# Two weight-chunk scalings moved to other places in VectorE's stream, and the first row tile normalized in two pieces

## The chip, the cores, the metric

One core of a Trainium2 chip. The metric is the device time of one execution in microseconds (us); medians of several executions are quoted. All kernels gave correct results.

## The reference

```
xn = layernorm(x)                                  # x: 2048 x 640, bf16
q  = xn @ wq                                       # 640 x (32 heads x 192)
s  = softmax(q @ k^T / sqrt(192)) @ v              # the last 512 keys of each head
s  = s @ wo                                        # (32 x 192) x 640
g  = silu( (sigmoid(xn @ w_gate) * (xn @ w_up)) @ w_down )
out = x + s * g
```

## The kernel before

The kernel computes the gated block first (from about 15 us), then the query projection of the first head group (from 164 us), then score and value phases of one head group after another, and the output products at the end. Query weights are cut into five chunks per group (one per 128 rows of wq). Before a chunk of the second group can be used it is scaled by one instruction, on VectorE for the chunks that matter here, and then combined into four sums by GpSimd:

```python
def scale_raw(g, c, on_act=True):
    raw = raw_t[g, c][:]
    if on_act:
        nc.scalar.activation(raw.bitcast(F16), raw, AF.Copy, scale=w_up)
    else:
        nc.vector.tensor_scalar(raw.bitcast(F16), raw, w_up, None, op0=ALU.mult)   # the row L221

def second_w(c):                                   # all of it on GpSimd
    copy_w(1, c, nc.gpsimd.tensor_copy)
    sum_w(1, c, nc.gpsimd.tensor_tensor, nc.gpsimd.tensor_copy)
    load_raw(1 + (c + 3) // NCD, (c + 3) % NCD, nc.gpsimd)
```

Where these stand in the stream is decided by two loops. `slots` are the parts of the first query projection; `stage_s` is one score tile, and `q_list` holds the next group's query parts that are woven between the score tiles:

```python
for n, k in enumerate((0, 1, 7, 2, 3, 8, 4, 5, 9, 6, 10)):
    slots[k]()
    ...
    elif n == 6:
        scale_raw(1, 2, on_act=False)              # third chunk: amid the projection
    if n in (0, 1, 6):
        second_w(min(n, 2))
...
        for k, x in enumerate(s_list):             # 16 score tiles
            stage_s(r, *x, k)
            ...
            if r == 0 and k in (3, 7):             # fourth and fifth chunk
                scale_raw(1, 3 + k // 4, on_act=False)
                second_w(3 + k // 4)
```

The normalization of a row tile is one VectorE instruction (`tensor_scalar`, 128x640), ahead of five transposes on TensorE.

All sixteen row tiles end in `finish`, which takes an output buffer from a pool of four ("fout"), multiplies by the gate, adds, and writes to HBM. Of the last eight some have their addition on GpSimd, and the last of all is done in three pieces (comments added in this cut and the ones above):

```python
def finish(ps, gB_sb, t, d0, d1, on_pool=False, queue=nc.sync):
    o_sb = late["fout"].tile([P, D], BF16, name="o_sb")      # "fout": 4 buffers in turn
    d = slice(d0, d1)
    if on_pool:
        tmp = late["tmp"].tile([P, D], F32, name="tmp")
        nc.vector.tensor_tensor(tmp[:, d], ps, gB_sb[:, d], ALU.mult)
        nc.gpsimd.tensor_tensor(o_sb[:, d], tmp[:, d], acc[t][:, d], ALU.add)
    else:
        nc.vector.tensor_tensor(ps, ps, gB_sb[:, d], ALU.mult)       # last multiplication
        nc.vector.tensor_tensor(o_sb[:, d], ps, acc[t][:, d], ALU.add)   # last addition
    queue.dma_start(of[t * P:(t + 1) * P, d], o_sb[:, d])
```

Each call takes the next buffer of the ring. The third piece of the last row tile therefore gets the buffer of the fourth user before it, a whole row tile whose addition was on GpSimd, and its own addition waits until that tile's 160 KB are written (in the profile before they land 1.78 us after the issue, at 899.48 us, and the addition starts at 899.66).

The softmax here doesn't subtract the row's maximum and nothing guards it: scores larger than these inputs give would overflow.

## Time and profile before

| | kernel before |
|---|---|
| time, median of 3 runs | 905.09 us (904.78 to 905.09) |
| span of the profiled run | 902.9 us |
| busy: TensorE, VectorE, ScalarE, GpSimd | 99%, 72%, 48%, 20% |
| first product of the gated block | 14.80 us |
| first query product, second score phase | 164.18 us, 209.63 us: 45.45 us apart |

The lines that carry this are in the prediction below. One view that I did not show there, because I did not look at it closely enough, is the chain of work that ended last, in order of time. Its end in the kernel before (start, duration, what):

```profile
896.13 1.55 POOL o_sb L726
897.68 0.02 issue
897.70 1.78 DMA out_dram<-o_sb
899.48 0.03 DVEq L729
...
899.66 0.29 DVE o_sb L729
```

The last addition is released by an output write, not by TensorE. The margin is small: in VectorE's timeline the last multiplication starts 0.45 us before it.

```profile
899.21 0.29 DVE L728 TENSOR_TENSOR ps_all<-ps_all,gBa_sb 128x128 f32<-128x128 f32 x1
899.66 0.29 DVE L729 TENSOR_TENSOR o_sb<-ps_all,acc_hi 128x128 bf16<-128x128 f32 x1 [0.16 <-DVE ps_all L728]
```

### The profile page before, as it was taken

How to read it: one execution, taken by the hardware profiler on the slowest of the kernel's cores; microseconds unless marked ns; L12 is line 12 of the kernel's file. 1: busy time of each engine (PE TensorE's matmuls, PEld its weight loads, DVE VectorE, ACT ScalarE, POOL GpSimd, SP SyncE). 2: the span in 40 equal slices, each digit the busy share in tenths (PEclk: the TensorE clock that was granted, in tenths of full speed). 3: DMA queues.
4: the chain of work that ended last, by engine and by line, in shares of the span. 5: the costliest groups of instructions: out<-in, count | busy, mean ns of one | idle time of the engine just before them, and what ended most of it. 6: DMA issues, size and time to landing. Idle time of an engine off the chain costs nothing. (4 is left out here: it accounts for less than half of the span.)

```text
span 902.9 us, 18554 instructions
## 1 busy us (share of the span) xinstructions
PE 896.0 (99%) x7791; PEld 531.6 (59%) x7791; DVE 653.0 (72%) x1090; ACT 432.9 (48%) x511; POOL 178.8 (20%) x220
## 2 busy tenths in 40 slices
PE   9999999999999999999999999999999999999998
PEld 5545454556656565656565656566666666565665
DVE  5879956677677867786778677866786678666566
ACT  4323346764247633753376437643854285424240
POOL 0051112780001100110011001100110000001982
PEclk9999999999999999999999999999999999999999
DMA  9993384424554645373626362727293815263744
GB/s 284 269 268 92 97 146 104 119 55 87 87 91 59 144 76 102 60 143 69 109 56 147 57 119 46 157 54 123 31 172 45 132 23 129 39 120 130 159 128 121
DMA packets 188069, 100.38 MB, mean 111 GB/s; under 512 B 156176, under 2 KB 180368, under 8 KB 187984
## 3 DMA queue, kind: packets, MB, share of 16 engines
q1 hardware_dynamic: 158656, 57.69, 32.5%
q0 software_dynamic: 9408, 29.93, 14.2%
q10 hardware_dynamic: 19920, 11.57, 5.5%
q8 instruction: 61, 1.00, 0.5%
q14 instruction: 24, 0.20, 0.1%
HBM read 57.87 MB, written 5.24 MB: 70 GB/s over the span
## 5 line engine op out<-in xcount | busy, mean ns | idle before, releaser
L657 ACT ACTIVATE E<-ps_all 128x1024 bf16<-128x1024 f32 x256 | 252.7, 1022 | 303.0 <-PE ps_all L653 184.8
L714 PE MATMUL ps_all<-wo_g,oT 128*128 128x512 bf16 (+2 forms) x1542 | 228.3, 299 | 0.0
L653 PE MATMUL ps_all<-qT,kT 64*128 64x512 bf16 x1536 | 194.4, 376 | 0.0
L671 PE MATMUL ps_all<-v_sb,E 128*128 128x193 bf16 x2048 | 189.8, 247 | 0.1
L671 PEld LDWEIGHTS <-E 128*128 128x128 bf16 x2048 | 168.6, 98 | 18.7 <-issue 6.8
L714 PEld LDWEIGHTS <-oT 128*128 128x128 bf16 x1542 | 121.5, 98 | 78.4 <-issue 2.3
L584 DVE COPY qp<-ps_all 128x512 f32<-128x512 f32 x150 | 100.7, 688 | 58.4 <-PE ps_all L563 58.3
L601 DVE TENSOR_TENSOR qT<-ps_all,qp 128x512 bf16<-128x512 f32 x165 | 109.7, 688 | 45.7 <-PE ps_all L563 37.4
L653 PEld LDWEIGHTS <-kT 64*128 64x128 bf16 x1536 | 75.4, 94 | 89.2 <-issue 5.2
L678 DVE TENSOR_TENSOR o_st<-ps_all,rden 128x768 bf16<-128x768 f32 x120 | 114.9, 957 | 5.0 <-DMA oT<-o_st 0.9
L202 POOL DMA_DIRECT2D raw<-in_A_wq_dram x80 | 48.1, 606 | 276.2 <-ACT wB L224 238.9
L135 POOL DMA_DIRECT2D k_sb<-in_A_k_cache_dram x32 | 32.7, 1026 | 275.2 <-DVE o_st L678 155.6
L219 ACT ACTIVATE raw<-raw,w_sc 128x1536 f16<-128x1536 bf16 x37 | 58.3, 1575 | 1.9 <-DMA raw<-in_A_wq_dram 1.0
L497 PE MATMUL ps_all<-wd_sb,hT_sb 128*128 128x512 bf16 (+1 forms) x384 | 52.8, 299 | 0.0
L563 PE MATMUL ps_all<-XA,wA 64*128 64x512 f16 x420 | 51.9, 376 | 0.2 <-DVE qp L584 0.2
L563 PE MATMUL ps_all<-XB,wB 64*128 64x512 f16 x420 | 52.0, 376 | 0.0
L563 PE MATMUL ps_all<-X,w 64*128 64x512 bf16 x420 | 51.9, 376 | 0.0
L749 DVE TENSOR_TENSOR acc_lo<-ps_all,acc_lo 128x640 f32<-128x640 f32 x48 | 39.5, 823 | 15.9 <-PE ps_all L714 15.7
L453 DVE TENSOR_TENSOR hT_sb<-ps_all,sig_sb 128x512 bf16<-128x512 f32 x48 | 32.4, 683 | 22.0 <-ACT sig_sb L452 11.3
L677 DVE RECIPROCAL rden<-ps_all 128x4 f32<-128x4 f32 x128 | 23.2, 181 | 34.1 <-PE ps_all L671 32.7
L452 ACT ACTIVATE sig_sb<-ps_all 128x512 bf16<-128x512 f32 x48 | 28.0, 596 | 40.1 <-PE ps_all L447 37.1
L749 DVE TENSOR_TENSOR acc_hi<-ps_all,acc_hi 128x640 f32<-128x640 f32 x48 | 39.3, 819 | 7.7 <-PE ps_all L714 7.7
(118 smaller groups left out, 764.0 us busy)
## 6 DMA issues: line engine op xcount, KB each, us to landing
raw<-in_A_wq_dram POOLq DMA_DIRECT2D x80, 192.0 KB, 4.1
k_sb<-in_A_k_cache_dram POOLq DMA_DIRECT2D x32, 192.0 KB, 5.6
wo_g<-in_A_wo_dram ACTq DMA_DIRECT2D x6, 960.0 KB, 7.1
v_sb<-in_A_v_cache_dram ACTq DMA_DIRECT2D x28, 192.0 KB, 3.8
gB_d<-gB_sb POOLq DMA_DIRECT2D x16, 160.0 KB, 3.5
gBa_sb<-gB_d SPq DMA_DIRECT2D x16, 160.0 KB, 3.9
xa_sb<-in_A_x_dram SPq DMA_DIRECT2D x16, 160.0 KB, 3.9
out_dram<-o_sb SPq DMA_DIRECT2D x15, 160.0 KB, 1.9
```

The lines of the kernel that those rows point to most:

```text
L202: eng.dma_start(raw[r], wq_r[:, c, :, g * GC:(g + 1) * GC])
L219: nc.scalar.activation(raw.bitcast(F16), raw, AF.Copy, scale=w_up)
L497: nc.tensor.matmul(oB_ps[:, d0:d0 + dsz], lhsT=hT_sb[:, f, q * P:(q + 1) * P], rhs=wd_sb[:, f, d0:d0 + dsz], start=(f == 0), stop=(f == NF ...
L563: nc.tensor.matmul(ps_all[:, b, :], lhsT=w(r, c), rhs=x[r, c, :], start=(first and k == 0), stop=(k == len(cs) - 1), skip_group_check=True,)
L584: nc.vector.tensor_copy(dst, part(b))
L601: nc.vector.tensor_tensor(q_out(i, u, pp), part(b), t, ALU.add)
L653: nc.tensor.matmul(ps[:, b, :], lhsT=kT[h, c * PC + j, :], rhs=qT_t[r][i, j][h, pp, :], start=(j == 0), stop=(j == PC - 1),)
L657: nc.scalar.activation(E_t[r, i, pp][:, c, :, :], ps, AF.Exp, scale=scale_qk)
L671: nc.tensor.matmul(o_ps[:, q // 2, q % 2, 0:DH + 1], lhsT=E[:, c, h, q * P:(q + 1) * P], rhs=vt[:, c, 0:DH + 1], start=(c == 0), stop=(c = ...
L678: nc.vector.tensor_tensor(o_st[:, :, h * DH:(h + 1) * DH].rearrange("p (b i) d -> p b i d", b=2), o_ps[:, :, :, 0:DH], rden[:].to_broadcas ...
L714: nc.tensor.matmul(oA[:, d0 - base:d0 - base + dsz], lhsT=oT_t[r, i, pp][:, q * PC + j, :], rhs=wo_t[runs[r][1]][:, cc, d0:d0 + dsz], star ...
L749: nc.vector.tensor_tensor(acc[t][:], oA[:, 0:D], acc[t][:], ALU.add)
```

## The change

Its intent: take the scalings of the third and fifth chunk away from places where TensorE waits for VectorE right behind them, and let TensorE's first transposes start before the whole first row tile is normalized. The line numbers of the changed kernel are 2 higher than before in what follows it (L563 becomes L565, L729 becomes L731).

```diff
         def ln_apply(t):
             xn = xpool.tile([P, D], BF16, name="xn")
-            nc.vector.tensor_scalar(
-                xn[:], x_tiles[t], mv[:, t, 0:1], rstd[:, t, :],
-                op0=ALU.subtract, op1=ALU.mult,
-            )
+            cuts = [0, 2 * P, D] if t == 0 else [0, D]
+            for d in map(slice, cuts, cuts[1:]):
+                nc.vector.tensor_scalar(
+                    xn[:, d], x_tiles[t][:, d], mv[:, t, 0:1], rstd[:, t, :],
+                    op0=ALU.subtract, op1=ALU.mult,
+                )
             return xn
@@
-        elif n == 6:
-            scale_raw(1, 2, on_act=False)
-        if n in (0, 1, 6):
-            second_w(min(n, 2))
+        if n < 2:
+            second_w(n)
+    scale_s = {0: 2, 3: 3, 15: 4}
@@
-            if r == 0 and k in (3, 7):
-                scale_raw(1, 3 + k // 4, on_act=False)
-                second_w(3 + k // 4)
+            if r == 0 and k in scale_s:
+                scale_raw(1, scale_s[k], on_act=False)
+                second_w(scale_s[k])
```

## The prediction

> **What bounds the kernel now.** I read the page first (busy shares, slices, the chain that ended last), then the waits of TensorE, then the timeline of the two stretches that the diff touches: the query projection and first score phase (164 to 211 us) and the head (1 to 12 us).
>
> The page: TensorE is busy 896.0 of 902.9 us, in every slice, at full granted clock. The slice row and the engine row say the same thing from two sides.
>
> ```profile
> span 902.9 us, 18554 instructions
> PE 896.0 (99%) x7791; PEld 531.6 (59%) x7791; DVE 653.0 (72%) x1090; ACT 432.9 (48%) x511; POOL 178.8 (20%) x220
> PE   9999999999999999999999999999999999999998
> PEclk9999999999999999999999999999999999999999
> ```
>
> So the change can give back only gaps on TensorE. The waits of TensorE name four. The third and fourth belong to the query products; the first two to the head.
>
> ```profile
> PE ps_all L350 <- DVE warm L344: 1.3, 1, 1.3
> PE ps_all L563 <- DVE qT L601: 0.4, 1, 0.4
> PE ps_all L360 <- ACT X L375: 0.3, 1, 0.3
> PE ps_all L563 <- DVE qp L584: 0.2, 1, 0.2
> ```
>
> These idle figures are too small, because the ends of matmuls are modelled and stretch into the gap; starts are the safe thing to subtract. In the timeline of TensorE, ten half-height matmuls take 1.08 us from start to start and twelve take 1.29 or 1.30 (next fence, a later score phase of the same shape, with nothing in its way).
>
> ```profile
> 223.02 1.24 PE L563 MATMUL ps_all<-X,acc_hi 64*128 64x512 bf16 x10
> 224.10 1.46 PE L653 MATMUL ps_all<-qT,kT 64*128 64x512 bf16 x12
> 225.40 1.24 PE L563 MATMUL ps_all<-XA,acc_hi 64*128 64x512 f16 x10
> ```
>
> Now the stretch of the change: the timeline of VectorE and TensorE, with the two scaling instructions of L221 that the diff moves.
>
> ```profile
> 172.01 1.29 DVE L601 TENSOR_TENSOR qT<-ps_all,acc_lo 128x512 bf16<-128x512 f32 x2 [3.07 <-PE ps_all L563]
> 173.22 0.61 DVE L221 TENSOR_SCALAR raw<-raw,w_sc 128x1536 f16<-128x1536 bf16 x1
> 173.74 3.08 DVE L601 TENSOR_TENSOR qT<-ps_all,acc_lo 128x512 bf16<-128x512 f32 x5
> ...
> 173.90 1.33 PE L563 MATMUL ps_all<-XC,wC 64*128 64x512 bf16 x10
> 175.68 0.80 PE L563 MATMUL ps_all<-XC,wC 64*128 64x512 bf16 x5 [0.45 <-DVE qT L601]
> ...
> 190.66 1.26 DVE L221 TENSOR_SCALAR raw<-raw,w_sc 128x1536 f16<-128x1536 bf16 x1
> 191.84 0.68 DVE L584 COPY qp<-ps_all 128x512 f32<-128x512 f32 x1
> ...
> 190.92 1.47 PE L653 MATMUL ps_all<-qT,kT 64*128 64x512 bf16 x12
> 192.57 1.25 PE L563 MATMUL ps_all<-XA,wA 64*128 64x512 f16 x10 [0.18 <-DVE qp L584]
> ```
>
> Gap one: the ten products start at 173.90, so the split ones could start at 173.90 + 1.08 = 174.98; they start at 175.68, 0.70 late. Gap two: 190.92 + 1.30 = 192.22 against 192.57, 0.35 late. Both stand right behind a scaling on VectorE that sits ahead of a read of PSUM for which TensorE is waiting.
>
> [...] the three scalings have one shape, yet take 0.61, 0.89 and 1.26 us. At 173.22 GpSimd was issuing loads; the one at 190.66 met a GpSimd product that ran from 190.59 to 191.50, and 191.50 + 0.42 is its end.
> [...] The wait at 175.68 is that: the split product writes the bank that the first add of the preceding slot reads.
> [...] The trace before has no cut one of this kind; its 128x640 normalization takes 0.44 us and lets the next instruction start after 0.36 (4.72 to 5.08).
>
> **The change part by part.** Count of work: VectorE gets one instruction more, all else keeps its count; the order of instructions on TensorE, ScalarE and GpSimd does not change. Everything is a matter of where three waits end.
>
> Third chunk, from the middle of the projection to the first score tile. Without the scaling at 173.22 the five adds behind it, which start every 0.60 us, can follow the two at 172.01 directly. The third add waits for TensorE (171.74 + 1.08 for its ten products, + 0.20 us until TensorE's end is seen = 173.02) and for VectorE, free at 172.01 + 1.20 = 173.21. So the adds start at 173.21, 173.81, 174.41 where they started at 173.74, 174.34, 174.94. The one at 174.41 reads the bank of the split product; it ends 0.69 later, 175.10, and TensorE goes on 0.05 later (as 175.63 led to 175.68): 175.15. Gain 0.53 us; 0.17 of the gap stays, because the adds themselves are behind. What follows hangs on the split product: it runs 0.65, ScalarE copies one half (0.60), VectorE adds (0.69), and the first product of the next tile waits for that add; before, 175.68 led to 177.75, 2.07 us, where TensorE alone needs 0.65 + 1.30 = 1.95. I keep the 2.07: 177.22. So 0.53 is passed on whole.
> The scaling itself now falls behind the last add, at about 177.1. VectorE is idle there: the row of the copy at 179.03 says 1.32 us before it. A scaling of 0.61, or up to 1.26 if it meets GpSimd, must be done by 179.03 - 0.53 = 178.50; in the worse case it meets a GpSimd copy that ends at 177.60 and ends at about 178.1. Cost 0. GpSimd needs the chunk at 181.12, so that doesn't wait either.
>
> Fourth chunk: stays behind the fourth score tile (183.69, 0.89 us), no gain. Moving 0.53 earlier it meets GpSimd at another point, at worst ending near 184.6; the two copies behind it then end at 185.8, and TensorE wants those banks at 186.38 - 0.53 = 185.85. Cost 0, by a hair.
>
> Fifth chunk, from behind the eighth score tile to behind the sixteenth. The 1.26 us at 190.66 are gone, the copy at 191.84 starts at about 190.66, and TensorE no longer waits: gain 0.35. At its new place VectorE has done its last add at about 199.45 - 0.88 = 198.57, and the first reciprocal of the value phase comes at 200.47 - 0.88 = 199.59, after 1.02 us of idle time in the row before. GpSimd has nothing to do then (it waits for this very chunk), so the scaling takes 0.61: 199.2, hidden. GpSimd's own five products and copies of this chunk slip from 195.80 to about 199.2 and, at 5.9 us for a chunk, end near 205.1; the load behind them is issued by 206.4. TensorE first reads the chunk in the next score phase, which starts at 209.63 - 0.88 = 208.75, some 2 us into it (fifth of five chunks). Margin over 4 us. Cost 0.
>
> First row tile in two pieces of 256 and 384. The intent is that TensorE's first two transposes begin before the whole row is normalized. Starts of the head, from its timeline: normalization 4.72, transposes 5.23, two warming products 5.74, first real product 6.54; the chain on VectorE and ScalarE beside it: statistics 5.08, aggregate 5.61, square root 5.85, copy of the turned tile 6.05 (0.36 us for the first part). The first piece may end 0.1 to 0.2 us before 5.17. The copy on ScalarE is behind the square root of the second tile, which is behind the statistics that VectorE does after both pieces, so it gets not earlier but later[...]. Then the wait of TensorE at 8.54 (0.26 us, for the copy of the second tile) moves later by as much. But the head has two anchors behind it: VectorE waits 0.53 us for a row tile at 8.11, which doesn't move, and TensorE's transposes at 9.21 wait for what VectorE does after it, while TensorE's products before them end at 8.54 + 10 x 0.056 = 9.10. So 0.11 us of delay is swallowed. Net 0[...].
>
> Sum: 0.53 + 0.35 - 0 = 0.88 us, passed to the end because TensorE has no wait after 192.57.
>
> **The rivals.** A: the third chunk's scaling at the head of the score phase becomes a new wait, since it sits ahead of the copy at 179.03. For: it is the same mechanism as before, and GpSimd is at work. Against: 1.32 us of idle time. If it did, up to 0.3 us come back: 904.5. B: GpSimd's late fifth chunk makes TensorE wait in the second score phase. For: 3.4 us later on the slowest engine. Against: the margin of over 4 us. If I had the margin wrong by 2 us more, the gain is lost and the time is 905 to 906. C: the split normalization helps TensorE for good, as its author hopes, by [...] a copy that was waiting for transposes. Against: the copy starts exactly 0.20 us after the square root in all tiles (5.85 to 6.05, 7.61 to 7.81, 9.83 to 10.03). For: 0.1 to 0.2 us at most, 904.0. D: noise. The three runs before spread over 0.31 us, a third of the effect.
>
> **Range and chances.** 905.09 - 0.88 = 904.2 us. Down to 903.6 if the head gains 0.2 and the runs fall low; up to 905.0 if half of the gain returns in a new wait. 2% are 18 us, twenty times the sum of all gaps in question, so within 2% is almost sure; what is left goes to a wait that I didn't see.
>
> **What would show it.** Right: no wait of TensorE on L563 of more than 0.2 us; the split product 1.25 us behind the start of the ten before it instead of 1.78; twelve score products ahead of the XA products of the third block in 1.30 us instead of 1.65; the L221 row with all three starts at new places, none followed by idle time on TensorE; GpSimd's last query-weight product near 205 us. Wrong: a wait of TensorE on VectorE between 177 and 179 or 184 and 187 (rival A), one on GpSimd after 208 (B), a first product at L360 earlier and the start of the row at 14.80 earlier as well (C).

The forecast's sum was 0.53 + 0.35 - 0 = 0.88 us, and it stands, since its two gains are worked out from starts and durations in the trace before. Its third term, the head, was counted as 0. Without the cut estimate that 0 is the author's guess: the trace before shows the slack of 0.11 us for it (9.21 - 9.10), but not that the copy on ScalarE gets later, nor by how much; the changed kernel's trace showed that afterwards (0.18 us). The 0.1 to 0.2 us by which the first piece "may end" sooner, which rival C and the range use, are an estimate as well, not worked out there: by share of elements it would be at most 384/640 of the 0.44 us, 0.26 us.

Two other numbers in it come from the traces like this. The 0.42 us by which a scaling ends after the GpSimd product that it met is seen twice before: 191.50 + 0.42 is the end of the one of 1.26 us, and the product that ran from 183.25 to 184.16 us is followed by the end of the one of 0.89 us at 184.58. The 0.20 us "until TensorE's end is seen": ten products that start at 177.75 take 1.08 us, and the copy that waits for them starts at 179.03.

## The result and the profile after

The changed kernel took 904.70 us (904.44 to 905.03, 6 runs), the kernel before 904.88 us (904.63 to 905.09, 6 runs) in the same rounds. The ratio is 0.9998, with a 95% interval of 0.9985 to 1.0011: the same. Here and below a ratio is the mean time of one kernel's runs over that of the kernel before in the same rounds, so it is not quite the ratio of the medians. The time lies in the predicted range, but only about a fifth of the predicted 0.88 us arrived: 0.18 us between the medians. So the question is where the rest went. That the time lies in the range (903.6 to 905.0) proves nothing: the 904.88 us of the kernel before lie in it too.

The page of the changed kernel:

```profile
span 902.9 us, 18555 instructions
PE 895.2 (99%) x7791; PEld 531.2 (59%) x7791; DVE 652.4 (72%) x1091; ACT 432.8 (48%) x511; POOL 179.0 (20%) x220
```

TensorE is busy 0.8 us less, with the same work, and yet the span is what it was. VectorE has 1091 instructions where it had 1090. The waits of TensorE, where four were listed before:

```profile
PE ps_all L352 <- DVE warm L346: 1.3, 1, 1.3
PE ps_all L362 <- ACT X L377: 0.7, 2, 0.4
```

Both waits for VectorE in the query products are gone; the one for ScalarE, in the head, has grown from 0.3 to 0.7 us. TensorE's timeline in the stretch of the change:

```profile
173.95 2.05 PE L565 MATMUL ps_all<-XC,wC 64*128 64x512 bf16 x15
175.64 1.65 PE L655 MATMUL ps_all<-qT,kT 64*128 64x512 bf16 x12
177.27 1.04 PE L565 MATMUL ps_all<-X,w 64*128 64x512 bf16 x8
...
190.43 1.48 PE L655 MATMUL ps_all<-qT,kT 64*128 64x512 bf16 x12
191.73 1.26 PE L565 MATMUL ps_all<-XA,wA 64*128 64x512 f16 x10
```

The view joins the fifteen XC products in one line; in the trace's records the split product, the eleventh, starts at 175.19, which is 1.24 us behind the first (predicted 1.25; before 1.78), so 0.16 us of the gap is still there (predicted 0.17). The next tile's first product starts at 177.27 (predicted 177.22), and twelve score products take 191.73 - 190.43 = 1.30 us to the next ones (predicted 1.30). The timeline of VectorE has the three scalings in their places:

```profile
172.06 4.28 DVE L603 TENSOR_TENSOR qT<-ps_all,acc_lo 128x512 bf16<-128x512 f32 x7 [3.07 <-PE ps_all L565]
...
177.13 0.82 DVE L221 TENSOR_SCALAR raw<-raw,w_sc 128x1536 f16<-128x1536 bf16 x1
178.54 0.69 DVE L586 COPY qp<-ps_all 128x512 f32<-128x512 f32 x1 [0.59 <-PE ps_all L565]
...
183.20 0.61 DVE L221 TENSOR_SCALAR raw<-raw,w_sc 128x1536 f16<-128x1536 bf16 x1
...
198.53 0.61 DVE L221 TENSOR_SCALAR raw<-raw,w_sc 128x1536 f16<-128x1536 bf16 x1
199.63 0.18 DVE L679 RECIPROCAL rden<-ps_all 128x4 f32<-128x4 f32 x1 [0.49 <-PE ps_all L673]
```

The first and the third are followed by idle time of VectorE that ends with TensorE, and TensorE's list of waits has none for VectorE behind any of the three, so none is in the way. The second score phase starts at 208.79 us instead of 209.63; counted from the first query product (164.22 and 164.18) the stretch is 44.57 us instead of 45.45. That is 0.88 us less, the predicted sum to the hundredth. The last multiplication on VectorE still has this: 898.41 us, against 899.21 before. Then the end of VectorE's timeline:

```profile
898.41 0.29 DVE L730 TENSOR_TENSOR ps_all<-ps_all,gBa_sb 128x128 f32<-128x128 f32 x1
899.94 0.29 DVE L731 TENSOR_TENSOR o_sb<-ps_all,acc_hi 128x128 bf16<-128x128 f32 x1 [1.25 <-issue]
```

Between these two neighbours 1.54 us pass, where it was 0.45. All of the gain is lost in this one place. The chain of work that ended last, to be set beside the one of before:

```profile
895.33 1.55 POOL o_sb L728
...
896.90 1.80 DMA out_dram<-o_sb
898.70 1.15 issue
899.85 0.05 DVEq L731
899.90 0.04 issue
899.94 0.29 DVE o_sb L731
```

GpSimd's addition and the issue of the write come 0.80 us earlier than before, as everything does. The write seems to take 1.80 us, and then there are 1.15 us called "issue", time in which the engine waits for nothing that the view knows. The view of the DMA traffic, asked for the 0.4 us in which this write is issued, tells more. Before, and after (issue, size, time from issue to landing):

```profile
out_dram<-o_sb SPq DMA_DIRECT2D x1, 160.0 KB, 1.8
```

```profile
out_dram<-o_sb SPq DMA_DIRECT2D x1, 160.0 KB, 2.9
```

The write itself landed 1.1 us late. In the trace's records it has sixteen landings, here called its parts, and sixteen packets of 4 bytes, which in these two profiles start 0.3 to 0.4 us before them in all but the late case. The records: before, all sixteen land 1.60 to 1.78 us after the issue; after, fifteen land 1.60 to 1.79 us after it and the sixteenth at 2.87. The chain of waits took the fifteenth for the end, hence the "issue". The addition started only after the last of the sixteen: at 899.94 us, with the sixteenth landing at 899.77 and the fifteenth at 898.69.

What held the sixteenth? One packet of another kind lies there in the trace: 8192 bytes on a queue that the profile marks "instruction", here called the fetch. It runs from 898.42 to 898.75 us, and the late part's 4-byte packet starts at 898.75, where the other fifteen started from 898.17 to 898.31. Before, the fetch's data run from 899.26 to 899.79 us and the last of the sixteen 4-byte packets starts at 899.12. So the fetch may account for the late start of that packet (0.43 us), but not for all of the delay: the late part landed 1.02 us after its packet started, the other fifteen 0.34 to 0.39 us after theirs. For those 0.65 us more the trace shows no cause.

### The profile page after: what moved, and what is told of

The parts are those of the page before. It is cut to its first block, busy times and chain, and to the rows that moved or that the text cites. A ratio compares the mean times of both kernels' runs of the same rounds, so it can differ in the third digit from the quotient of the medians. Undisturbed runs are those within 1.5% of the kernel's fastest.

```text
span 902.9 us, 18555 instructions
## 1 busy us (share of the span) xinstructions
PE 895.2 (99%) x7791; PEld 531.2 (59%) x7791; DVE 652.4 (72%) x1091; ACT 432.8 (48%) x511; POOL 179.0 (20%) x220
## 5 line engine op out<-in xcount | busy, mean ns | idle before, releaser
L565 PE MATMUL ps_all<-XB,wB 64*128 64x512 f16 x420 | 52.0, 376 | 0.0
L565 PE MATMUL ps_all<-X,w 64*128 64x512 bf16 x420 | 51.9, 376 | 0.0
L565 PE MATMUL ps_all<-XA,wA 64*128 64x512 f16 x420 | 51.9, 376 | 0.0
```

The lines of the kernel that those rows point to most:

```text
L565: nc.tensor.matmul(ps_all[:, b, :], lhsT=w(r, c), rhs=x[r, c, :], start=(first and k == 0), stop=(k == len(cs) - 1), skip_group_check=True,)
```

## Experiments

Theory I: the cutting of the first row tile gives VectorE one instruction more. By that, its instruction fetch near the end falls a little earlier against the output write that the last addition waits for, and gets ahead of one of its sixteen completions. It is the count that matters and not what the instruction does. Rivals: noise (II); an earlier end of the kernel brings the write and the fetch together whatever the count, so that the scalings themselves cause it (III); the pieces cause it through what they do to the head (H).

r1 to r12: each has 4 to 6 timed runs (r7 and r8 have 4, r6 has 6, the changed kernel's result 6). The table gives medians, the mean less the mean of the kernel before in the same rounds, and from the profiled run: the stretch from first query product to second score phase, the time from the start of the last multiplication to that of the last addition, the landing of the fifteenth and sixteenth part after the write's issue, and the span less the start of the first product of the gated block. The last column leaves out the head, because the time of that product varied from 14.80 to 15.19 us among four executions of one and the same head. The cause is the load of an early row tile: VectorE starts the statistics of that tile between 8.11 and 8.78 us in eleven of the fourteen profiles, right after waiting for its load, and in each of these the first product of the gated block follows 6.69 us later. (In the other three, the changed kernel, r4 and r5, it follows 6.93 us or more later, and something else sets it.)

| kernel | VectorE instr., buffers | median us | mean less before | stretch | mult. to add. | parts 15, 16 | span less head |
|---|---|---|---|---|---|---|---|
| before | 1090, 4 | 904.88 | | 45.45 | 0.45 | 1.75, 1.78 | 888.05 |
| changed | 1091, 4 | 904.70 | -0.17 | 44.57 | 1.54 | 1.79, 2.87 | 888.08 |
| r1 changed again | 1091, 4 | 904.60 | -0.21 | 44.57 | 1.52 | 1.78, 2.85 | 887.77 |
| r2 changed | 1091, 5 | 903.88 | -0.83 | 44.57 | 0.32 | 1.78, 2.76 | 887.13 |
| r3 before | 1090, 5 | 904.63 | -0.13 | 45.47 | 0.32 | 1.78, 2.88 | 888.01 |
| r4 scalings only | 1090, 4 | 903.93 | -0.85 | 44.57 | 0.44 | 1.75, 1.78 | 887.15 |
| r5 changed, memset moved | 1090, 4 | 906.14 | +1.16 | 44.57 | 0.44 | 1.74, 1.77 | 887.46 |
| r6 scalings only, again | 1090, 4 | 904.27 | -0.65 | 44.57 | 0.45 | 1.75, 1.78 | 887.36 |
| r7 pieces only | 1091, 4 | 905.86 | +0.96 | 45.45 | 1.53 | 1.78, 2.85 | 888.71 |
| r8 fifth chunk only | 1090, 4 | 904.84 | +0.01 | 45.10 | 0.45 | 1.74, 1.78 | 887.90 |
| r9 scalings, one memset more | 1091, 4 | 904.55 | -0.30 | 44.57 | 1.52 | 1.78, 2.85 | 887.76 |
| r10 third chunk only | 1090, 4 | 904.10 | -0.86 | 44.63 | 0.45 | 1.74, 1.78 | 887.02 |
| r11 scalings only | 1090, 5 | 903.76 | -1.24 | 44.57 | 0.32 | 1.79, 2.86 | 886.69 |
| r12 before, one memset more | 1091, 4 | 905.73 | +0.80 | 45.48 | 1.51 | 1.78, 2.84 | 888.65 |

The kernel before had 904.72 us (904.59 to 905.05, 9 runs) beside r1 to r4, 904.79 (10 runs, these nine and one more) beside r5 to r8, and 904.94 (904.43 to 905.36, 9 runs) beside r9 to r12. The sizes are tenths of a microsecond, and most intervals include 1.

### r1: the changed kernel again

No edit. Expected: 

> The changed kernel itself, once more, to see whether its lost gain is the same in another execution. In its first profile TensorE reached the last output products 0.81 us earlier than before, and the last add of VectorE then stood 1.25 us waiting until the sixteenth part of an earlier row tile's write (the first user of the same output buffer) landed, 1.08 us after the other fifteen. Theory S (a systematic late part: the fetch of instructions by DMA falls on that write each time): the profile shows a wait of 1 us or more before the last add again, and the time is 0.0 to 0.3 us under before. Theory C (chance of that one execution): no such wait in this profile, the span is about 902.1, and the timed runs spread in two groups about 0.8 us apart.

Ratio 0.9998 (0.9985 to 1.001). The end of VectorE's timeline shows the same wait, in another execution:

```profile
899.84 0.29 DVE L731 TENSOR_TENSOR o_sb<-ps_all,acc_hi 128x128 bf16<-128x128 f32 x1 [1.23 <-issue]
```

So the late part is not an accident of one profile.

### r2: the changed kernel with five output buffers

```diff
-("fout", 4)
+("fout", 5)
```

Expected: 

> The changed kernel with five output buffers in place of four, so that the last piece of the last row tile uses a buffer whose write was long done. Theory T (the gain is lost in the tail, in the wait of the last add for that write): the wait before the last add is at most 0.2 us, and the time is 0.7 to 1.1 us under before, about 904.0. Rival (the gain of TensorE is not passed on because something else bounds the tail, such as the writes at the end or fixed work after them): the time stays within 0.3 us of before.

Ratio 0.9990 (0.9977 to 1.0004), 0.83 us off the mean: the predicted gain is there once the last addition no longer waits for that write. The sixteenth part is still late (2.76 us), and nothing waits for it. This shows that the wait for the buffer is what the gain was lost to.

### r3: the kernel before with five output buffers

The same edit on the kernel before. Expected: 

> The kernel before with five output buffers: the control for the run with the changed kernel. In its profile the last add waited only some 0.1 us for the same write beyond its own input (899.48 against 899.50), so theory T expects 0.0 to 0.2 us under before. If it were 0.5 us or more under before, the buffer alone would be the gain and not what the change does.

Ratio 0.9998 (0.9986 to 1.0011): the buffer alone brings 0.13 us, the 0.45 us that become 0.32. So r2's gain is not the buffer's own. The control also gave something that theory I had not foreseen: with five buffers the sixteenth part is late (2.88 us) with 1090 instructions too. So with five buffers the count alone does not decide. What does go with the late part here is the moment of the fetch: its data end 1.84 us after the write's issue in r3 (1.82 in r11), as in the late cases with four buffers. Why five buffers move the fetch was not tested.

### r4: the scalings without the pieces

```diff
-            cuts = [0, 2 * P, D] if t == 0 else [0, D]
+            cuts = [0, D]
```

Expected: 

> The changed kernel with the first row tile normalized in one piece, so only the two scalings moved. The prediction's sum: TensorE starts the second score phase 0.83 to 0.88 us earlier than before (209.63), so about 208.77; the head is the same as before. Theory T with a systematic late part that comes from this timing: the same wait before the last add, time 0.0 to 0.3 us under before. Rival (the added VectorE instruction shifts where instructions are fetched, and so makes the part late): no wait, time 0.7 to 1.0 us under before.

Ratio 0.9991 (0.9978 to 1.0003), 0.85 us off the mean. The end of VectorE's timeline is that of the kernel before, with all of it earlier:

```profile
898.49 0.29 DVE L730 TENSOR_TENSOR ps_all<-ps_all,gBa_sb 128x128 f32<-128x128 f32 x1
898.94 0.29 DVE L731 TENSOR_TENSOR o_sb<-ps_all,acc_hi 128x128 bf16<-128x128 f32 x1 [0.15 <-DVE ps_all L730]
```

Rival III falls: the earlier end alone brings no late part. What the two pieces do, as seen so far, is to cancel the gain of the scalings.

### r5: the changed kernel with a memset moved to GpSimd

```diff
-        nc.vector.memset(eps_t[:], eps)
+        nc.gpsimd.memset(eps_t[:], eps)
```

The pieces stay, but VectorE has 1090 instructions again. Expected: 

> The whole change, with four buffers, but the small memset of the epsilon goes from VectorE to GpSimd, so VectorE has as many instructions as before (1090 in place of 1091). Theory I (one VectorE instruction more moves the last fetch of its instructions onto the write that the last add waits for): no part of that write is late, the last add waits at most 0.2 us, and the time is 0.7 to 1.0 us under before, about 903.9. Rival H (the two pieces of the first row tile bring the late part by their timing, whatever the count): wait above 1 us, time 0.0 to 0.3 us under before.

The time missed the expectation: ratio 1.0014 (1.0001 to 1.0028), 1.16 us over the kernel before. The timeline of ScalarE says why. In the changed kernel, and then in r5:

```profile
0.74 1.28 ACT L368 ACT_TABLE_LOAD   x1 [0.74 <-PEq L851]
4.19 0.29 ACT L368 ACTIVATE rstd<-mv,eps_t 128x1 f32<-128x1 f32 x1 [2.16 <-DVE mv L329]
```

```profile
4.24 1.28 ACT L368 ACT_TABLE_LOAD   x1 [4.24 <-DVE mv L329]
5.53 0.29 ACT L368 ACTIVATE rstd<-mv,eps_t 128x1 f32<-128x1 f32 x1
```

The square root's table load used to run before the statistics were there; now it stands behind the wait for them, and the head is 1.3 us later. I had not thought of that side effect. The tail is as theory I expects: 0.44 us from multiplication to addition, no late part, although the row tile is cut. Rival H is weakened, but with a head this different it is not a clean test.

### r6: by my mistake, r4 a second time

Expected: 

> Placeholder of intent: see kernel. The two moved scalings alone plus one more VectorE instruction in the head that computes nothing new (the epsilon's memset done twice; 1091 on VectorE). Theory I: the late part is back, the last add waits above 1 us, time 0.0 to 0.3 us under before. Rival H: no late part, time 0.7 to 1.0 us under before, as without the extra instruction.

The text is for a kernel with one memset more. The kernel was that of r4, unchanged, so the text can't be held against it; the intended kernel is r9. As a repeat of r4 it is useful: ratio 0.9993 (0.998 to 1.0005), 0.65 us off the mean, no late part.

### r7: the pieces without the scalings

The first part of the diff alone, on the kernel before. Expected: 

> The kernel before with only the first row tile in two pieces (1091 instructions on VectorE, no scaling moved). The prediction's sum: 0 at the end of the head, so TensorE reaches the second score phase at 209.6 as before. Theory I: the late part falls on the write, the last add waits about 1.2 us, and the time is 0.4 to 0.9 us over before. Rival H without the late part: within 0.2 us of before.

Ratio 1.0011 (0.9997 to 1.0025), 0.96 us over the kernel before, with the late part. In the profiled run 0.67 us of its 1.3 us over the span before are the head (the load named above):

```profile
899.69 0.29 DVE L730 TENSOR_TENSOR ps_all<-ps_all,gBa_sb 128x128 f32<-128x128 f32 x1
901.22 0.29 DVE L731 TENSOR_TENSOR o_sb<-ps_all,acc_hi 128x128 bf16<-128x128 f32 x1 [1.24 <-issue]
```

### r8: the fifth chunk alone

```diff
-            if r == 0 and k in (3, 7):
-                scale_raw(1, 3 + k // 4, on_act=False)
-                second_w(3 + k // 4)
+            if r == 0 and k in (3, 15):
+                scale_raw(1, 3 + k // 15, on_act=False)
+                second_w(3 + k // 15)
```

Expected: 

> The kernel before with only the fifth chunk's scaling moved to the end of the first score phase (1090 on VectorE). The prediction's term: twelve score products ahead of the third block's XA products in 1.30 us in place of 1.65, so the stretch from the first query product (164.18) to the second score phase (209.63) shrinks by 0.35 us, from 45.45 to 45.10; the gap of 0.70 us at the split product stays. Theory I: no late part, time 0.2 to 0.5 us under before.

The stretch is 45.10 us, 0.35 less, as the prediction has it for this chunk; the wait of TensorE in the XC products is still there:

```profile
174.25 1.33 PE L563 MATMUL ps_all<-XC,wC 64*128 64x512 bf16 x10
176.02 0.80 PE L563 MATMUL ps_all<-XC,wC 64*128 64x512 bf16 x5 [0.44 <-DVE qT L601]
```

The time (ratio 1.0000, 0.9987 to 1.0014) does not show the 0.35 us. In the profiled run the first product of the gated block was 0.34 us later than in the profile before (the load named above came 0.35 us later), and the stretch from the last addition to the end 3.45 us instead of 3.19. Four runs can't settle an effect of this size: inconclusive in the time, clear in the trace.

### r9: the scalings and one memset more

On top of r4, the memset of the epsilon tile (128x1, at the start) is done twice on VectorE. No row tile is cut.

```diff
         nc.vector.memset(eps_t[:], eps)
+        nc.vector.memset(eps_t[:], eps)
```

Expected: 

> The kernel that the run before last of this name was meant to be: the two scalings moved, the first row tile in one piece, and the memset of the epsilon tile on VectorE (128x1, at the very start) done twice, so VectorE has 1091 instructions as in the changed kernel, but no normalization is cut. Theory I (one VectorE instruction more shifts an instruction fetch onto the output write that the last addition waits for): one of the sixteen parts of that write lands about 1 us behind the others, the last addition starts more than 1.2 us (1.3 to 1.6) behind the start of the last multiplication of VectorE instead of 0.45, and the median is 0.0 to 0.4 us under the kernel before. Rival H (the pieces themselves cost it, by when the head runs): no late part, 0.45 us between the two, and 0.5 to 1.0 us under the kernel before. Query products to second score phase 44.57 us in both.

Ratio 0.9996 (0.9984 to 1.0009), 0.30 us off the mean. The end of VectorE's timeline:

```profile
898.07 0.29 DVE L731 TENSOR_TENSOR ps_all<-ps_all,gBa_sb 128x128 f32<-128x128 f32 x1
899.59 0.29 DVE L732 TENSOR_TENSOR o_sb<-ps_all,acc_hi 128x128 bf16<-128x128 f32 x1 [1.23 <-issue]
```

As theory I expects and rival H does not.

### r10: the third chunk alone

The kernel before with the third chunk's scaling behind the first score tile; the fourth and fifth stay (`scale_s = {0: 2, 3: 3, 7: 4}`). Expected: 

> The kernel before with only the third chunk's scaling moved to the beginning of the first score phase; the fourth and fifth where they were; 1090 VectorE instructions. By the prediction's step for the third chunk the stretch from the first query product to the second score phase falls from 45.45 to 44.92 us (0.53 less), with no new wait between 177 and 179 us. If the third step was mis-sized and the fifth made up for it, it would differ by more than 0.05. By theory I no late part at the end: 0.45 us from the last multiplication to the last addition, and a median about 0.5 us under the kernel before, less or more 0.4 for the head.

The time: ratio 0.9990 (0.9978 to 1.0003), 0.86 us off the mean. But the stretch is 44.63 us, 0.82 less and not 0.53. The timelines of GpSimd, VectorE and TensorE around the fifth chunk's scaling, which is at its old place here:

```profile
190.16 0.91 POOL L237 TENSOR_TENSOR acc_hi<-raw 128x384 f16<-128x384 f16 x1
```

```profile
190.52 0.96 DVE L221 TENSOR_SCALAR raw<-raw,w_sc 128x1536 f16<-128x1536 bf16 x1
191.40 0.68 DVE L584 COPY qp<-ps_all 128x512 f32<-128x512 f32 x1
```

```profile
190.78 1.48 PE L653 MATMUL ps_all<-qT,kT 64*128 64x512 bf16 x12
192.13 1.26 PE L563 MATMUL ps_all<-XA,wA 64*128 64x512 f16 x10
```

TensorE goes from the score products to the XA products in 1.35 us, where it took 1.65 before. The scaling takes 0.96 us instead of the 1.26 of before: everything on VectorE came earlier against GpSimd, so it meets GpSimd's products at another point. The prediction's arithmetic for such a meeting fits: the product ends at 191.07, plus 0.42 is 191.49, and the scaling ends at 191.48. So of the second gap's 0.35 us, 0.29 or 0.30 close by themselves when the third chunk moves. The gains of the two moves are 0.82 and 0.35 alone and 0.88 together.

### r11: the scalings with five output buffers

Both edits of r2 and r4. Expected: 

> The two scalings moved, the first row tile in one piece, and five output buffers instead of four: the candidate for the fastest. By theory I it keeps the whole 0.88 us and the last addition waits for no output write: stretch 44.57 us, 0.32 us from the last multiplication to the last addition, median 0.8 to 1.1 us under the kernel before (about 903.8). If the fifth buffer brings nothing once the extra instruction is gone, it equals the scalings alone within 0.15 us.

The fastest: 903.76 us (903.32 to 903.96, 5 runs), ratio 0.9987 (0.9973 to 1.0001), 1.24 us off the mean. The wait before the last addition is gone:

```profile
898.18 0.29 DVE L730 TENSOR_TENSOR ps_all<-ps_all,gBa_sb 128x128 f32<-128x128 f32 x1
898.50 0.29 DVE L731 TENSOR_TENSOR o_sb<-ps_all,acc_hi 128x128 bf16<-128x128 f32 x1
```

It was a little better than expected. Against r4 and r6 the span less head is 0.46 and 0.67 us shorter; 0.12 or 0.13 of that lie between multiplication and addition, and 0.33 behind the last addition (3.05 us to the end instead of 3.38), which I can't explain.

### r12: the kernel before with one memset more

The edit of r9 and nothing else. Expected: 

> The kernel before with nothing changed but the epsilon tile's memset on VectorE done twice: 1091 VectorE instructions, about 0.06 us of work before any data has come. Theory I: a late sixteenth part of the output write and 1.3 to 1.6 us from the last multiplication to the last addition, median 0.7 to 1.2 us over the kernel before, as the pieces alone gave. Rival H (the pieces themselves, not the count): nothing, within 0.3 us of the kernel before and 0.45 us from multiplication to addition.

Ratio 1.0009 (0.9996 to 1.0021), 0.80 us over the kernel before (in the profiled run 1.21 us, of which 0.61 us are the head, where the load came late). The start of VectorE's timeline shows the whole edit:

```profile
0.93 0.06 DVE L263 MEMSET eps_t<- 128x1 f32 x1
1.06 0.06 DVE L264 MEMSET eps_t<- 128x1 f32 x1
```

and its end, 900 us later, what it costs:

```profile
899.59 0.29 DVE L729 TENSOR_TENSOR ps_all<-ps_all,gBa_sb 128x128 f32<-128x128 f32 x1
901.10 0.29 DVE L730 TENSOR_TENSOR o_sb<-ps_all,acc_hi 128x128 bf16<-128x128 f32 x1 [1.22 <-issue]
```

An instruction of 0.06 us, which runs two microseconds before the first row tile is there, does what the two pieces do. Rival H falls.

### What the experiments settle, and what not

With four buffers, the five profiles with 1091 VectorE instructions (changed, r1, r7, r9, r12) all have the late part and 1.51 to 1.54 us from multiplication to addition; the six with 1090 (before, r4, r5, r6, r8, r10) have none and 0.44 or 0.45. The five have the pieces or a memset, the scalings or not. So, with four buffers, the count, or the position of the instructions behind it, is the cause, and noise, the scalings and the pieces as such are not.

The net cost is less than the 1.08 us of the late landing, because what follows the last addition was shorter in these runs (2.96 to 2.99 us to the end, against 3.19 to 3.45 in the six others). In spans less head, the kernel before and its likes: 888.71 and 888.65 against 888.05, so 0.63 us; with both scalings moved: mean 887.87 (changed, r1, r9) against 887.26 (r4, r6), so 0.61 us. Of the 0.88 us about 0.6 are given back. The timed means, which include the head, say the same less sharply: with the late part 0.88 us more on the kernel before (mean of r7 and r12), 0.52 us more with both scalings moved (changed, r1, r9 against r4, r6).

The link in between, the fetch, is seen but not tested. The records don't name the engine that a fetch is for. That VectorE's count moves one of them can be seen elsewhere in the same traces: one fetch starts at 728.5 to 729.8 us in all six profiles with 1091 instructions, and at 732.2 to 733.8 us in all eight with 1090, with four buffers and with five. In every late case, with five buffers too, the late part's packet starts where the fetch's data end, with one exception that the trace does not explain (r2, where the fetch runs earlier). The fetch's data end 1.79 to 1.85 us after the write's issue in all eight late cases, with four buffers and with five, and 2.09 to 2.15 us after it in the six others; the last of sixteen undisturbed 4-byte packets starts 1.42 us after the issue. The data's first byte differs less: 1.50 to 1.53 us after the issue in the late cases (r2: 1.05), 1.56 or 1.82 to 1.84 in the others. The shift of the end by about 0.3 us is of the size of one step of VectorE there (starts at 898.55, 898.94, 899.21 in the kernel before: 0.39 and 0.27 us), as if the fetch were set off one instruction sooner; that is an inference. What sets it off exactly, and why a completion is held back that by its fifteen neighbours was due before the fetch's first byte, stays open, and so do the 0.65 us by which its landing follows its packet later than the others do.

The page of the profile before has two queues of the kind "instruction": q8 with 61 packets and 1.00 MB, and q14 with 24 packets and 0.20 MB, in the trace 8192 bytes each and most of them tens of us apart. This fetch, on q14, costs time by the inference above where the count of VectorE's instructions is 1091 and the buffers are four: the completion behind it lands 1.08 us behind its fifteen neighbours (2.87 against 1.79 us in the changed kernel).

## Why the prediction was right or wrong, point by point

- **What bounds the kernel, and the two gaps.** Right: the starts-only reading gave 0.70 and 0.35 us, and the waits are gone from the list.
- **Third chunk, 0.53 us.** The chain of starts is right (next tile's first product at 177.27 for 177.22, and in r10 the copy behind it is 0.53 us earlier against the first query product). The scaling at its new place took 0.82 us and met GpSimd, as the worse case allowed, and was hidden: VectorE then idled 0.59 us. Rival A did not happen. Incomplete: the move also closes most of the second gap, which the prediction did not look for (r10: 0.82).
- **Fifth chunk, 0.35 us.** Right as a move alone (r8: 0.35) and right in the sum, but not as the second of two: with the third moved it brings 0.06.
- **Fourth chunk, 0.** Right, without the hair's breadth: it took 0.61 us, though a GpSimd product ran until 183.31 us when it started at 183.20; GpSimd's next product took 1.19 us where it took 0.91 before.
- **GpSimd's late fifth chunk, 0.** Right: its products ran from 199.21 to 204.80 us (predicted about 199.2 to 205.1) and TensorE waits for nothing there. Rival B did not happen.
- **Two pieces, 0 in the head.** Right in the size, with one reading wrong. TensorE's first transposes began 0.07 us earlier (5.16 for 5.23), but its first real product 0.10 us later (6.64 for 6.54), because the chain of VectorE and ScalarE came 0.18 us later (the square root of the second tile at 6.03 for 5.85). The prediction said later, but the size that it gave was not shown by any trace. VectorE's timeline has the size:

```profile
4.71 0.64 DVE L339 TENSOR_SCALAR xn<-x_sb,mv,rstd 128x256 bf16<-128x256 bf16 x2
5.26 0.49 DVE L324 BATCH_NORM_STATS2 stats<-x_sb 128x6 f32<-128x320 bf16 x1
```

  The two let the statistics start after 0.55 us, where the one instruction took 0.36. The prediction took the row tile at 8.11 us for an anchor that doesn't move. It moves between executions, from 7.91 us in the changed kernel's profile to 8.78 us in r7, and in r1, r2 and r7 (8.37 to 8.78 us) it hides the pieces' delay whole, the first product following 6.69 us later as without pieces. In the changed kernel's own profile the tile came 0.20 us earlier than before and did not set the head, so its 14.84 for 14.80 us does not show how much was swallowed. Rival C did not happen.
- **The sum, "passed to the end because TensorE has no wait after 192.57".** This is the step that failed: the path from TensorE's last wait to the end of the kernel. It is true of TensorE, which kept 0.81 us to its last products, but the end is not TensorE's: behind the last products come a multiplication and an addition on VectorE, and the addition waits for an output write. The chain of waits of the kernel before said so, with the write ending 0.18 us before the addition. With that margin a delay of the write goes straight to the last addition (sixteenth landing 2.87 us after the issue for 1.78, addition 1.54 us after the multiplication for 0.45), and the cut row tile brought one. The prediction counted "VectorE gets one instruction more" and gave it no cost outside the head; it cost about 0.6 us net, 900 us later.
- **The range.** That 904.70 us fell in it is luck: the prediction started from 905.09 us (three runs), the kernel before had 904.88 us in the rounds of the result, and the range was wide enough to hold the kernel before too, that is, no gain at all.

What would show the prediction wrong was listed as new waits between 177 and 187 us, after 208, and in the head. The wait that came was in none of them.

## What to carry to other kernels

When TensorE is 99% busy and the change is worth tenths of a microsecond, read the last ten entries of the chain of waits as carefully as the stretch that you change: what ends the program can be a write that a recycled buffer waits for, and one buffer more takes it off the path (here 1.52 or 1.54 us from the last multiplication to the last addition became 0.32, in r2). Test every part of a change alone and in company: one part here undid the others at the other end of the program, and two gains were not additive because moving one scaling changed where the other met GpSimd (its 1.26 us became 0.96, in r10). An edit that adds a trivial instruction can cost more than its duration (in r12 0.06 us, against 0.60 us more of span less head), so a control that adds an idle instruction is worth one run.
